# Results of the stage between two loops: kept in tiles that outlive its pools, stored from the sync queue, the dO store first

## The chip, the cores and the metric

One core of a Trainium2 chip runs the whole kernel in one launch. The metric is the device time of the program in microseconds. The core has five engines that run beside each other: TensorE (PE, matmuls), VectorE (DVE), ScalarE (ACT), GpSimd (POOL) and SyncE (SP), which here issues transfers only. Transfers (DMA) are issued into a queue by SP, ACT or POOL and carried out by 16 DMA engines.

## The reference

The kernel computes the forward pass and all gradients of one transformer block with conditional layer norms: 2048 tokens, width D = 512, 32 heads of 16, a hidden layer of 1792 with a squared ReLU.

```
mod = silu(c) @ w_mod                       # six rows: sa, ca, ga, sb, cb, gb
h   = layernorm(x) * (1 + ca) + sa
q, k, v = h @ wqkv                          # 32 heads
o   = softmax(q k^T / 4) v
x1  = x + ga * (o @ wo)
h2  = layernorm(x1) * (1 + cb) + sb
out = x1 + gb * (relu(h2 @ w1 + b1)**2 @ w2 + b2)
```

Ten outputs leave the kernel. Those that matter here are out_0 (the result `out`), out_3 (the gradient of `wo`, 512 x 512), and sums over all tokens that the gradients of `c` and `w_mod` are made of. The gradient of `wo` is O^T times da, where O is the attention's output for all tokens and da the gradient that reaches `o @ wo`. The gradient that reaches O is called dO.

## The kernel before

The program has four stages, one after the other: the first layer norm with the projection to q, k and v; the **forward loop** over attention, into which the dense work (the two layer norms, the hidden layer and its gradients) of the first three quarters of the tokens is woven; a **stage between the loops**, in which the last quarter (512 tokens, chunk c = 3) goes through the dense work with nothing beside it; and the **backward loop** over attention, 64 pairs of blocks, each block with sixteen exponentials, followed by the last weight gradients.

The stage between the loops is `last_chunk`. Its order is written out by hand (`manual_schedule`): each engine runs its instructions in the order of the code. Work can be put off: `later(lag, f, ...)` adds an entry to the list `due`, to be done `lag` ticks on, and `tick()`, called between groups of matmuls, runs what has come due. `run_due(True)` at the end runs all that is left. `sp(to, fro)` issues a transfer on the sync queue, in the order of these calls. [...]

What the stage leaves, in the order in which the arithmetic makes it:

- `dOs_c`, the dO of this chunk, token-major; four transposes (DMA) turn it into `dOT`, and `store_grad` stores `dOT` in `dOT_st` and the softmax correction `dlt`, transposed to `dltT`, in `d_st`, from where later heads of the backward loop load them. The first head's share of the last quarter is made on TensorE instead (`head_do`), so the loop can start without these stores.
- `x1_c` and `xlast`, the result of three and of one token tiles, stored to out_0.
- The gradient of `wo`, in four row blocks (`add_chain` with idx from FC + 4*NS = 34 on). The sum over the first three chunks was kept in DRAM and has been fetched ahead; VectorE adds the last chunk's matmul to it and writes the result to a slot (L381), and a store issued from ScalarE one tick later (L335) brings it to out_3.
- The four row sums, in one PSUM bank (`rsums`), copied by VectorE to `racc` (L1225) and stored as four rows to `rows_st` (L1272). They are needed at the end of the program only.

The tiles live in pools: `wk`, `ffw` (racc, and dwbuf with the slots), `cb` (dOT, x1_c, dOs_c). These pools close with the stage, and the backward loop's pools get the same memory. The framework then makes the first instruction that writes to a new tile wait for all that still reads the old ones, stores included. Such first writers are the exponential that fills `E_u` (L1339), the product `dS_u` (L1353), the DMA transpose into `dsT` (L1366) and POOL's fill of the second head set (L945). Other tiles outlive the stage: `r_inv` (the softmax denominators, not read again after the stage), the first head set (k, v, q, do and `qs`, which is spread into `qz` in this stage and free after that), and the pool `dwr` (`dpad`, `proda`, `xlast`), which is released after the stage for POOL's later use.

[...]

In the backward loop, TensorE makes scores (L1333) in three PSUM banks, ScalarE the exponentials (L1339), TensorE the product dO V^T (L1351), VectorE dS (L1353), SP the transposes of dS (L1366), and TensorE accumulates the gradients of k and v (L1384, L1393) and q (L1411).

Of the kernel before, what the change touches and what calls it, by code (L numbers as in the profile page):

```python
# [17 lines left out]
BF = dt.bfloat16  # L18
F32 = dt.float32

P = 128
D = 512
DC = 4
H = 32
# [3 lines left out]
FC = 14  # L28
# [6 lines left out]
def kernel(  # L35
# [6 lines left out]
    n = A_x.shape[1]  # L42
# [3 lines left out]
    NS = -(-FC // 3)  # L46
# [3 lines left out]
    out0_v = out_0[0].rearrange("(t p) d -> p t d", p=P)  # L50
# [3 lines left out]
    DVE = nc.vector  # L54
    ACT = nc.scalar
    POOL = nc.gpsimd
    SP = nc.sync
# [18 lines left out]
    r_inv = persist.tile([P, TT, H], F32, name="r_inv")  # L76
# [3 lines left out]
    rows_st = dram.tile([11, D], F32, name="rows_st")  # L80
# [10 lines left out]
    dOT_st = dram.tile([D, n], BF, name="dOT_st")  # L91
    m_st = dram.tile([H, n], BF, name="m_st")
    d_st = dram.tile([H, n], BF, name="d_st")
# [51 lines left out]
    with ExitStack() as ph:  # L145
# [135 lines left out]
        for g in range(QC):  # L281
            cols = slice(512 * g, 512 * g + 512)
# [13 lines left out]
    with ExitStack() as ph:  # L296
# [7 lines left out]
        racc = ffw.tile([P, 5, D], F32, name="racc")  # L304
        pools = {}

        def mm():
            return pools["mm"].tile([P, 512], F32, name="pm", tag="pm")
# [18 lines left out]
        def later(lag, f, *args):  # L327
            due.append((unit[0] + lag, f, args))
# [10 lines left out]
        def part_tile(w, idx, load):  # L339
            part = cb.tile([P, 512], F32, name="part", tag="part", bufs=4)  # L340
            if load:
                sp(part[:, 0:w], p_st[idx][:, 0:w])
            return part
# [12 lines left out]
            else:  # L356
                ahead[idx] = part_tile(w, idx, True)[:, 0:w]

        slots = {"p": 0, "r": 0}

        def slot(kind, w):
            i = slots[kind]
            slots[kind] = i + 1
            if kind == "r":
                return L_dw[0][:, 512 * (i % 4):512 * (i % 4) + w]
            lo = 2048 + 768 * (i % 6)
            return L_dw[0][:, lo:lo + 2 * w].bitcast(F32)

        L_dw = []

        def add_chain(c, lag, idx, w, lhs, rhs, dst):
            def run():
                if final[0]:
                    acc = pools["mm"].tile([P, 512], F32, name="pc", tag="pc", bufs=3)
                else:
                    acc = mm()
                for ti in range(4):
                    PE.matmul(acc[:, 0:w], lhs(ti), rhs(ti), start=(ti == 0), stop=(ti == 3))  # L378
                if c == QC - 1:
                    res = slot("r", w)  # L380
                    DVE.tensor_tensor(res, acc[:, 0:w], ahead.pop(idx), ALU.add)  # L381
                    later(1, ACT.dma_start, dst, res)
                    if idx < FC - 4:
                        later(1, fetch_part, idx + 4)
                    elif idx < FC:
                        later(1, fetch_part, idx - FC + 4 + FC + 4 * NS)
                    elif idx + 6 < FC + 4 * NS:
                        later(1, fetch_part, idx + 6)
                    return
                if final[0]:  # L390
                    part = slot("p", w)
                    ACT.activation(part, acc[:, 0:w], AF.Identity)
                else:
                    part = part_tile(w, idx, False)[:, 0:w]
                    DVE.tensor_copy(part, acc[:, 0:w])  # L395
                if c == 0:
                    later(1, sp, p_st[idx][:, 0:w], part)
                else:
                    POOL.dma_start(out=p_st[idx][:, 0:w], in_=part, accum_op=ALU.add)
            return (unit[0] + lag, c, run, idx >= FC + 4 * NS)  # L400
# [271 lines left out]
            else:  # L672
                DVE.tensor_scalar(dlt[:, ti, :], delta[:], -1.0, None, ALU.mult)

        def store_grad(c, lag, dOT, dlt):
            dltT = wk.tile([P, P], BF, name="dltT", tag="dltT", bufs=1)
            later(lag, sp, dltT[:], dlt.rearrange("p t h -> p (t h)"), True)
            cols = slice(512 * c, 512 * c + 512)
            later(lag + 3, sp, dOT_st.rearrange("(b p) n -> p b n", p=P)[:, :, cols], dOT.rearrange("p b t q -> p b (t q)"))
            for ti in range(4):  # L680
                later(lag + 3, sp, d_st[:, 512 * c + ti * P:512 * c + (ti + 1) * P], dltT[H * ti:H * ti + H, :])

        funits = [(qc, hg, kt) for qc in range(QC) for hg in range(HG) for kt in range(TT)]
        fh, fe, fcur, fdone, dense = {}, {}, {}, [], []
# [250 lines left out]
        strm, hsets = [], []  # L935
# [33 lines left out]
        def fill(k):  # L969
            for _ in range(min(k, len(dwq))):  # L970
                next_chain()
# [4 lines left out]
        def last_chunk(O_c, L, w1T, w2T):  # L976
            c = QC - 1
            ts = slice(4 * c, 4 * c + 4)
            g_c, x1_c, gf_c, gfT, w1_nat = (L[key] for key in ("g", "x1", "gf", "gfT", "w1"))
# [71 lines left out]
            dpad = dwr.tile([P, 4, 4, 32], BF, name="dpad")  # L1051
# [61 lines left out]
            dlt = wk.tile([P, 4, H], BF, name="dlt", tag="dlt", bufs=1)  # L1113
# [99 lines left out]
            dOT = cb.tile([P, DC, 4, P], BF, name="dOT", tag="gfT")  # L1213
            for ti in range(4):
                later(1, sp, dOT[:, :, ti, :], dOs_c[:, ti, :], True)
            store_grad(c, 1, dOT, dlt)
            later(1, sp, keep["dOs"][:, ts, :], dOs_c[:])
            later(2, sp, out0_v[:, 4 * c:4 * c + 3, :], x1_c[:, 0:3, :])
            mlp(3, {5: head_do})
            fill(len(dwq))  # L1220
            dwq.extend(add_chain(c, 1, FC + 4 * NS + a, D, lambda ti, a=a: O_c[:, ti, a * P:(a + 1) * P], lambda ti: da_c[:, ti, :],
                                 out_3[a * P:(a + 1) * P, :]) for a in range(DC))
            fill(3)
            flush_sums(True)
            DVE.tensor_copy(racc[0:97, 0, :], pools["rs"][0:97, :])  # L1225
            fill(1)
            sp(out0_v[:, 4 * c + 3, :], xlast[:])
            run_due(True)
# [1 line left out]
        keep = {}  # L1230
        final[0] = True
        with ExitStack() as ph2:
            pools["mm"] = ph2.enter_context(tc.tile_pool(name="psM2", bufs=4, space=bass.MemoryType.PSUM))
            with tc.manual_schedule(engines={PE.engine, ACT.engine, DVE.engine, SP.engine, POOL.engine}):
                pools["rs"] = pools["mm"].tile([P, 512], F32, name="rsums", tag="rs", bufs=1)
                DVE.memset(pools["rs"][:], 0.0)
                unit[0] += 1
                run_due()
                L = loads["L"]
                L_dw.append(ffw.tile([P, FC * D], BF, name="dwbuf", tag="wB"))  # L1240
                vaugpool.release()
                head_set(0)
                DVE.memset(hsets[0]["q"][:], 0.0)
                DVE.memset(hsets[0]["do"][:], 0.0)
                copy_const(hsets[0]["k"][:], 1.0)
                O_c = late_finish()
                sp(L["gfT"].rearrange("p t o q -> p (t o) q"), flat(L["gf"]), True)
                for i in range(4):
                    fetch_part(i)
                att.close()  # L1250
                qzpool = tc.alloc_tile_pool(name="qzpool", bufs=1, side="right")
                qz = [qzpool.tile([P, TT, 4, 32], BF, name="qz0")]
                kpool = tc.alloc_tile_pool(name="kpool", bufs=1, side="right")
                dpool = tc.alloc_tile_pool(name="dpool", bufs=1, side="right")
                dwr = tc.alloc_tile_pool(name="dwr", bufs=1, side="right")
                w2T = kpool.tile([P, DC, FF], BF, name="w2T_1", tag="ks")
                for s in range(4):
                    sp(w2T[:, s, :], w2T_st[:, s, :])
                w1T = dpool.tile([P, FC, D], BF, name="w1T_1", tag="dt")
                for s in range(7):  # L1260
                    sp(w1T[:, 2 * s:2 * s + 2, :], w1T_st[:, 2 * s:2 * s + 2, :])

                def head_loads():
                    done = slice(0, 512 * (QC - 1))
                    for i, (to, fro) in enumerate(list(kvq_loads(0)) + list(row_loads(hsets[0]["do"][:, done], dOT_st, 0, done, d_st))):
                        later(i, sp, to, fro)
                    later(12, copy_const, qz[0].rearrange("p t h d -> p (t h d)"), 0.0)
                    later(16, spread_qz, 0)

                last_chunk(O_c, L, w1T, w2T)  # L1270
                for j, row in ((0, 5), (1, 3), (2, 4), (3, 2)):
                    SP.dma_start(out=rows_st[row:row + 1, :], in_=racc[32 * j:32 * j + 1, 0, :])  # L1272
        dwr.release()

    KS_tok, dOs_tok = keep["KS"], keep["dOs"]
# [11 lines left out]
    with ExitStack() as ph:  # L1287
# [162 lines left out]
        with tc.manual_schedule(engines={PE.engine, ACT.engine, DVE.engine, SP.engine, POOL.engine}):  # L1450
# [3 lines left out]
            for b in range(NU // 4 + 3):  # L1454
                toks, bank = order_t if on_pe(b - 1) else order_n
                for tok in toks:
                    c, i = tok[0], int(tok[1:] or 0)
# [22 lines left out]
                    elif c == "T" and 0 <= b - 1 < NU // 4:  # L1480
                        dst, pt = held.pop(i - 1)
# [9 lines left out]
    with ExitStack() as ph:  # L1491
# [156 lines left out]
        with tc.manual_schedule(engines={PE.engine, ACT.engine, DVE.engine}):  # L1648
            for k, (key, i) in enumerate(order):
                for g in range(2):  # L1650
# [4 lines left out]
                    for ti in range(8):  # L1655
                        t = 8 * g + ti
                        PE.transpose(pt[:, ti, :], xs[key, i][:, t * P:(t + 1) * P], identb[:])
                    if key == "dq":
                        dst = dq_tok[:, 8 * g:8 * g + 8, i * P:(i + 1) * P]
                    else:  # L1660
                        dst = dvk_tok[:, 8 * g:8 * g + 8, i, :]
# [32 lines left out]
            for b in range(3):  # L1694
                for ic in range(DC):
                    dwqkv(b, ic)
                    i = b * DC + ic
# [75 lines left out]
```

## Time and profile before

| | us |
|---|---|
| time, median of 3 runs (2641.7 to 2649.67) | 2642.49 |
| span of the profiled run | 2640.8 |
| TensorE busy | 2375.0 (90%) |
| ScalarE busy | 2322.8 (88%) |
| VectorE busy | 1750.3 (66%) |
| last addition of a wo gradient (L381) starts | 1207.27 |
| first exponential of the backward loop starts | 1213.44 |
| last exponential of the backward loop starts | 2505.3 |

Times within the span are microseconds from its start. A group of instructions is given with its line, engine, operation, tile written and tiles read, its count, its busy time and mean length, and then the time for which its engine stood idle just before it and what ended most of that. In the list of waits a line reads: engine and line that waited, what released it, total, times, longest. In the chain that ended last and in the timeline a line begins with its start and its length. The length of a transfer in the timeline is that of its issue alone; when it has landed is known from the completion records of the trace. Matmul records show their modelled ends.

### The profile page before, as it was taken

To read this page: it belongs to the slowest core of one execution; us is meant where nothing else is said; L and a number is where in the kernel's file an instruction comes from. 1 tells how busy PE (TensorE), PEld (TensorE's weight loads), DVE (VectorE), ACT (ScalarE), POOL (GpSimd) and SP (SyncE) were. 2 spreads that over 40 slices of the span, in tenths; PEclk is the share of its full clock that TensorE was granted. 3 is DMA by queue.
4 is the path that set the end of the run, shared out by engine and by line. 5 is a ranking of instruction groups with operands and counts; after the bars stand their busy time and mean duration, and the time that the engine had idled before them with its cause. 6 is when DMAs were issued, how large, how long until landed. Compare 5 with 4: busy or idle time off the path is not lost.

```text
span 2640.8 us, 48843 instructions
## 1 busy us (share of the span) xinstructions
PE 2375.0 (90%) x18110; PEld 746.7 (28%) x18183; DVE 1750.3 (66%) x2234; ACT 2322.8 (88%) x3594; POOL 362.9 (14%) x369
## 2 busy tenths in 40 slices
PE   6699989988988889898999999999999999999999
PEld 2211112322322222352222222222222222222343
DVE  7101134434444534567989989999998999989962
ACT  4599999998999999745999999999999999999943
POOL 2100010211242123201110101101011010110100
PEclk9755559997999799997989999999999999989999
DMA  8863366336855684888999999999999999999982
GB/s 242 195 153 119 99 155 138 85 111 158 137 103 115 140 146 94 193 254 173 196 199 193 205 194 203 197 194 199 198 202 188 199 187 198 195 189 208 194 242 83
DMA packets 1254801, 453.75 MB, mean 172 GB/s; under 512 B 1130127, under 2 KB 1225363, under 8 KB 1254306
## 3 DMA queue, kind: packets, MB, share of 16 engines
q1 hardware_dynamic: 1226066, 415.24, 80.1%
q0 software_dynamic: 10944, 16.78, 4.4%
q10 hardware_dynamic: 17552, 18.59, 2.5%
q8 instruction: 143, 2.34, 0.4%
q14 instruction: 96, 0.79, 0.1%
HBM read 97.08 MB, written 73.95 MB: 65 GB/s over the span
## 4 chain that ended last, share of the span: by engine, by line
PE 42%; ACT 40%; issue 6%; DVE 5%; DMA 2%; SPq 1%; ACTq 0%; POOL 0%; DVEq 0%; POOLq 0%
ACT E_u L1339 20%; ACT ET L704 16%; PE dqacc L1411 6%; PE psS_A L1333 4%; ACT dsT L1482 3%; PE accVK L1384 3%; PE psST L702 3%; PE psS_C L1333 3%; PE psS_B L1333 2%; PE accVK L1393 2%; PE pm L542 2%; PE pm L378 2%; PE oacc L718 2%; PE pdh L1597 2%; PE pwq L1631 2%
## 5 line engine op out<-in xcount | busy, mean ns | idle before, releaser
L1353 DVE TENSOR_TENSOR dS_u<-psD_u,E_u 128x1024 bf16<-128x1024 f32 x1024 | 1187.8, 1218 | 112.1 <-PE psS_B L1333 40.9
L704 ACT ACTIVATE ET<-psST 128x1024 bf16<-128x1024 f32 x1024 | 945.0, 1286 | 39.1 <-PE psST L702 38.4
L1339 ACT ACTIVATE E_u<-psS_A 128x512 bf16<-128x512 f32 x768 | 503.4, 655 | 28.6 <-DMA rows_st<-racc 12.1
L1339 ACT ACTIVATE E_u<-psS_B 128x512 bf16<-128x512 f32 x768 | 499.4, 650 | 5.4 <-issue 0.9
L702 PE MATMUL psST<-qt_sb,kt_sb 32*128 32x512 bf16 x2048 | 408.4, 464 | 67.7 <-ACT ET L704 33.0
L1351 PE MATMUL psD_u<-iv,ido 32*128 32x512 bf16 x2048 | 424.6, 400 | 0.2
L1339 ACT ACTIVATE E_u<-psS_C 128x512 bf16<-128x512 f32 x512 | 332.5, 649 | 1.5 <-PE psS_B L1333 0.7
L1333 PE MATMUL psS_A<-ik,iq 32*128 32x512 bf16 x768 | 305.7, 398 | 18.7 <-ACT E_u L1339 8.1
L1333 PE MATMUL psS_B<-ik,iq 32*128 32x512 bf16 x768 | 307.8, 401 | 10.4 <-ACT E_u L1339 3.2
L718 PE MATMUL oacc<-ET,vaug 128*32 128x512 bf16 x2048 | 246.7, 472 | 5.3 <-DVE ostage L722 5.3
L1384 PE MATMUL accVK<-dS_u,qz 128*32 128x512 bf16 x2048 | 227.9, 415 | 0.5 <-DVE dS_u L1353 0.3
L1333 PE MATMUL psS_C<-ik,iq 32*128 32x512 bf16 x512 | 196.3, 383 | 32.8 <-ACT dsT L1482 28.6
L1333 PEld LDWEIGHTS <-iq 32*128 32x128 bf16 x2048 | 127.3, 92 | 313.3 <-issue 299.0
L1393 PE MATMUL accVK<-E_u,dOs_tok 128*16 128x512 bf16 x2048 | 213.1, 406 | 0.0
L702 PEld LDWEIGHTS <-kt_sb 32*128 32x128 bf16 x2048 | 90.2, 94 | 399.6 <-issue 388.8
L1429 POOL TENSOR_TENSOR dQacc<-dQacc,dqtmp 128x512 f32<-128x512 f32 x64 | 81.3, 1270 | 881.3 <-ACT dqtmp L1424 881.3
L1411 PE MATMUL dqacc<-dsT,KS_tok 128*32 128x512 bf16 x2048 | 182.1, 465 | 14.0 <-DMA dsT<-dS_u 4.7
L722 DVE COPY ostage<-oacc 128x512 f32<-128x512 f32 x32 | 22.0, 689 | 229.8 <-PE oacc L718 182.1
L395 DVE COPY part<-pm 128x512 f32<-128x512 f32 (+2 forms) x103 | 63.5, 617 | 133.3 <-PE pm L378 126.7
L1482 ACT ACTIVATE dsT<-ptT 128x1024 bf16<-128x1024 bf16 x128 | 147.0, 1148 | 4.0 <-PE ptT L1374 3.8
L1351 PEld LDWEIGHTS <-ido 32*128 32x128 bf16 x2048 | 106.7, 91 | 111.2 <-issue 107.0
L1384 PEld LDWEIGHTS <-qz 128*32 128x32 bf16 x2048 | 60.9, 98 | 244.9 <-issue 231.8
(339 smaller groups left out, 2255.8 us busy)
## 6 DMA issues: line engine op xcount, KB each, us to landing
p_st<-part POOLq DMA_DIRECT2D x36, 256.0 KB, 5.2
kt_sb<-qkT_st SPq DMA_DIRECT2D x128, 64.0 KB
wA<-in_B_w_dram SPq DMA_DIRECT2D x28, 256.0 KB
dsT<-dS_u SPq DMA_TRANSPOSE x448
wB<-w1T_st SPq DMA_DIRECT2D x21, 256.0 KB
wA<-w2T_st SPq DMA_DIRECT2D x21, 256.0 KB
wB<-in_B_w_dram SPq DMA_DIRECT2D x21, 256.0 KB
p_st<-part POOLq DMA_DIRECT2D x25, 192.0 KB, 3.9
```

What stands on the lines that cost most here:

```text
L702: PE.matmul(ps[:, hi, :], kt_sb[r:r + 32, kt * P:(kt + 1) * P], qt_sb[r:r + 32, :], start=True, stop=True, tile_position=(r, 0))
L704: ACT.activation(ET[:, 2 * pair:2 * pair + 2, :], ps[:], AF.Exp, scale=SCALE)
L718: PE.matmul(oacc[32 * hq:32 * hq + 32, :], lhsT, ET[:, hq, :], start=(kt == 0), stop=(kt == TT - 1), tile_position=(0, 32 * hq), skip_grou ...
L1333: PE.matmul(psS[:], st["q"][r:r + 32, qt * P:(qt + 1) * P], st["k"][r:r + 32, kc * 512:kc * 512 + 512], start=True, stop=True, tile_positi ...
L1339: ACT.activation(bst[u][0][:, hq, :], sst.pop((u, hq))[:], AF.Exp, scale=SCALE)
L1351: PE.matmul(psD[:, hi, :], st["do"][r:r + 32, qt * P:(qt + 1) * P], st["v"][r:r + 32, kc * 512:kc * 512 + 512], start=True, stop=True, til ...
L1353: DVE.tensor_tensor(dS_u[:, 2 * pair:2 * pair + 2, :], psD[:], E_u[:, 2 * pair:2 * pair + 2, :], ALU.mult)
L1384: PE.matmul(cur["vk"][32 * hq:32 * hq + 32, :], hst[hg]["qz"][:, qt, hq, :], bst[u][1][:, hq, :], start=(qt == 0), stop=False, tile_positi ...
L1393: PE.matmul(acc[32 * hq:32 * hq + DH, :], dOs_tok[:, qt, (hg * 4 + hq) * DH:(hg * 4 + hq + 1) * DH], E_u[:, hq, :], start=False, stop=(qt ...
L1411: PE.matmul(acc[32 * hq:32 * hq + 32, :], KS_tok[:, kc * 4 + kt, h * DH:h * DH + 32], tT[:, :, hq * 4 + kt, :], start=(kt == 0), stop=(kt ...
L1429: POOL.tensor_tensor(dst2, dst, tmp[:], ALU.add)
L1482: ACT.activation(dst, pt[:], AF.Identity)
```

## The change

Three edits, all in the last microseconds of the stage between the loops.

1. The last results no longer lie in tiles of the closing pools. The four `wo` gradient blocks go to the two halves of the first head set's `qs`, to `dpad` and to a new tile `dwlast` in `dwr`; the row sums go to `r_inv`. A new kind of slot, "w", hands these out from the list `L_late`. The aim is that the first writers of the backward loop don't have to wait for these stores.
2. The stores of the `wo` gradient are issued on the sync queue (`sp`) instead of ScalarE's.
3. In the last chunk the store of `dOT` and those of `dltT` come due one tick after the transposes instead of three more (`more=1`), and the store of the three out_0 tiles comes first, then the copy of `dOs_c`, so that the dO stores are issued ahead of `xlast`, of the `wo` gradient and of the row sums.

```
         def slot(kind, w):
             i = slots[kind]
             slots[kind] = i + 1
+            if kind == "w":
+                return L_late[i]
...
                 if c == QC - 1:
-                    res = slot("r", w)
+                    late = idx >= FC + 4 * NS
+                    res = slot("w" if late else "r", w)
                     DVE.tensor_tensor(res, acc[:, 0:w], ahead.pop(idx), ALU.add)
-                    later(1, ACT.dma_start, dst, res)
+                    later(1, sp if late else ACT.dma_start, dst, res)
...
-        def store_grad(c, lag, dOT, dlt):
+        def store_grad(c, lag, dOT, dlt, more=3):
             dltT = wk.tile([P, P], BF, name="dltT", tag="dltT", bufs=1)
             later(lag, sp, dltT[:], dlt.rearrange("p t h -> p (t h)"), True)
             cols = slice(512 * c, 512 * c + 512)
-            later(lag + 3, sp, dOT_st.rearrange("(b p) n -> p b n", p=P)[:, :, cols], dOT.rearrange("p b t q -> p b (t q)"))
+            later(lag + more, sp, dOT_st.rearrange("(b p) n -> p b n", p=P)[:, :, cols], dOT.rearrange("p b t q -> p b (t q)"))
             for ti in range(4):
-                later(lag + 3, sp, d_st[:, 512 * c + ti * P:512 * c + (ti + 1) * P], dltT[H * ti:H * ti + H, :])
+                later(lag + more, sp, d_st[:, 512 * c + ti * P:512 * c + (ti + 1) * P], dltT[H * ti:H * ti + H, :])
...
-            store_grad(c, 1, dOT, dlt)
+            later(1, sp, out0_v[:, 4 * c:4 * c + 3, :], x1_c[:, 0:3, :])
             later(1, sp, keep["dOs"][:, ts, :], dOs_c[:])
-            later(2, sp, out0_v[:, 4 * c:4 * c + 3, :], x1_c[:, 0:3, :])
+            store_grad(c, 1, dOT, dlt, 1)
             mlp(3, {5: head_do})
             fill(len(dwq))
             dwq.extend(add_chain(c, 1, FC + 4 * NS + a, D, lambda ti, a=a: O_c[:, ti, a * P:(a + 1) * P], lambda ti: da_c[:, ti, :],
                                  out_3[a * P:(a + 1) * P, :]) for a in range(DC))
+            qs = hsets[0]["qs"].rearrange("p t e -> p (t e)")
+            L_late.extend((qs[:, 0:D], qs[:, D:2 * D], dpad.rearrange("p t h d -> p (t h d)"),
+                           dwr.tile([P, D], BF, name="dwlast", tag="proda")[:]))
             fill(3)
             flush_sums(True)
-            DVE.tensor_copy(racc[0:97, 0, :], pools["rs"][0:97, :])
+            keep["sums"] = r_inv.rearrange("p t h -> p (t h)")
+            DVE.tensor_copy(keep["sums"][0:97, :], pools["rs"][0:97, :])
...
                 for j, row in ((0, 5), (1, 3), (2, 4), (3, 2)):
-                    SP.dma_start(out=rows_st[row:row + 1, :], in_=racc[32 * j:32 * j + 1, 0, :])
+                    SP.dma_start(out=rows_st[row:row + 1, :], in_=keep["sums"][32 * j:32 * j + 1, :])
```

More of the change, by code (lines that the diff above doesn't have):

```diff
@@ L357, in fetch_part @@
                 ahead[idx] = part_tile(w, idx, True)[:, 0:w]
-        slots = {"p": 0, "r": 0}
+        slots = {"p": 0, "r": 0, "w": 0}
         def slot(kind, w):
@@ L367, in slot @@
             return L_dw[0][:, lo:lo + 2 * w].bitcast(F32)
-        L_dw = []
+        L_dw, L_late = [], []
         def add_chain(c, lag, idx, w, lhs, rhs, dst):
```

## The prediction

> **What bounds the kernel now.** I read the page first, for where the change can matter at all.
>
> ```profile
> PE 2375.0 (90%) x18110; PEld 746.7 (28%) x18183; DVE 1750.3 (66%) x2234; ACT 2322.8 (88%) x3594; POOL 362.9 (14%) x369
> ...
> L1339 ACT ACTIVATE E_u<-psS_A 128x512 bf16<-128x512 f32 x768 | 503.4, 655 | 28.6 <-DMA rows_st<-racc 12.1
> ```
>
> The span is TensorE and ScalarE work; the edited lines lie in none of the big groups. But the last line, the exponentials of the backward loop, has 28.6 us of idle time before it, of which 12.1 us end with a store of four row sums. The loop cannot start before that store has landed. The list of waits between 1195 and 1225 us shows that this is one wait, and who else stood still with it:
>
> ```profile
> ACT E_u L1339 <- DMA rows_st<-racc: 12.1, 1, 12.1
> ...
> PE psS_A L1333 <- ACT E_u L1339: 6.2, 2, 5.6
> ```
>
> ScalarE waits for the store and TensorE for ScalarE (its score banks are full); VectorE, in the same list, waits 6.9 us for TensorE. These are one gap, not three. The chain that ended last, in order of time, runs through it:
>
> ```profile
> 1207.27 0.69 DVE dwbuf L381
> 1207.98 3.21 DMA out_dram<-dwbuf
> ...
> 1211.76 1.14 DMA rows_st<-racc
> 1213.44 2.56 ACT E_u L1339 x5
> ```
>
> The arithmetic ends at 1207.27 + 0.69 = 1207.96. From there to 1213.44, 5.5 us, everything waits for stores. The timeline of the same stretch tells what the sync queue (SPq) did and when the first scores stood:
>
> ```profile
> 1195.90 5.45 SPq L325 DMA_TRANSPOSE dOT<-dOs_c  x4
> ...
> 1207.69 0.38 SPq L325 DMA_DIRECT2D dOT_st<-dOT  x1
> ...
> 1208.10 0.37 PE L1333 MATMUL psS_A<-ik,iq 32*128 32x512 bf16 x1 [0.95 <-DMA out_dram<-dwbuf]
> ...
> 1208.12 2.44 SPq L325 DMA_DIRECT2D d_st<-dltT  x4
> 1210.67 1.34 SPq L1272 DMA_DIRECT2D rows_st<-racc  x4
> ```
>
> The dO store is issued at 1207.69 though its transposes were issued by 1201.35; the four d_st stores take 2.44 us of issue time and the four row stores come last. The first scores stand at 1208.10 + 0.37 = 1208.47.
>
> **Why the exponential waits at all.** E_u takes memory of pools that close with this stage. The waits written into the built program for the first exponential name the last store of all of racc, dwbuf (three of the four wo gradient results), dOT, x1_c and dOs_c. In the changed build the same instruction names only the dO store, the out_0 store of three tiles, the copy of dOs_c and the four dO transposes: rows_st, d_st and out_3 are gone from its list. So after the change the dO store is the last thing that can hold it.
>
> [...] The completion records of this trace put dOT_st at 1211.28, 3.6 us after its issue[...]. [...] 0.34 us for one out_3 issue on ScalarE, 0.33 us for the out_0 store of the same 128 KB on sync. [...] Here the granted clock is 1.00 until 1210[...].
>
> **The change part by part.**
> *Row sums in r_inv, wo gradients in iqs, dpad and dwlast.* Five VectorE instructions keep their number and shape (0.57 to 0.69 us each) and only write elsewhere. iqs had its last reader at 1176.8 (the copy into qz, 1.05 us) and dpad at 1200.33 (its transposes, 0.39 us), four microseconds ahead of the first write at 1204.87: cost nothing. The waits for old dwbuf stores go; the three results already stood back to back with TensorE (matmuls 1203.10 to 1205.86), so gain nothing.
> *Four out_3 stores from ScalarE to sync.* ScalarE stood idle from 1201.4: no gain there. On sync 4 x 0.34 = 1.4 us, behind the dO store in order, so hidden from it. Ahead of what? Of the four row stores (1.34 us) and of the first dsT transpose of the loop.
> *dO store ahead.* New order on sync: x1_c store, dOs_tok copy, dltT transpose, dO store, d_st, xlast, out_3, rows. From 1201.35: 0.54 + 0.59 + 1.23 = 2.36 (the issue times these have in the timeline of before), so the dO store is issued at 1203.7 and off the queue at 1204.1 (0.38), 4.0 us earlier than before. Its inputs, the transposes, had landed by 1202.57 (completion records). Landing: 384 + 512 + 512 KB pass between 1201.9 and the end. Low end: 3.6 us from issue as before, 1207.3. High end: 1.44 MB at 244 GB/s (1195 to 1200 us) is 5.9 us[...], 1208.8. I take 1207.7, near the 342 GB/s of 1205 to 1207.5. From the landing of the row sums (1212.91) to the exponential (1213.44) there were 0.53 us, so the store allows a start between 1207.8 and 1209.3, 1208.2 as taken.
> *Does something else hold it?* Yes: the scores. The first score waits for the last wo gradient result (its PSUM bank), 1207.95, in both builds. Scores stand at 1208.47, exponential some 0.1 us later: 1208.6. So the start is the later of 1208.6 and 1208.2: 1208.6, between 1208.6 and 1209.3.
> *The tail on sync.* d_st wait for dltT, which now follows 896 KB in the queues: about 1206.3. Then 2.44 + 0.33 + 1.4 + 1.34 = 5.5 us: sync is free at 1211.8. The first dsT transpose was issued at 1217.32, 3.9 us after the first exponential; now it is wanted at 1212.5, so it still finds the queue free, with 0.7 us to spare. Its first reader, dqacc, comes two blocks of 16 exponentials later. POOL's fill of the second head set, behind dO, starts earlier; nobody needs it for 100 us.
> *Sum.* 1213.44 - 1208.6 = 4.8 us, 4.1 at the high end of the store. All of it is on the path, since all engines stood in this gap. 2642.5 - 4.7 = **2637.8 us**, 0.18% less.
>
> **What the loop makes of an earlier start.** The clock is the unknown. Windows of 10 us:
>
> ```profile
> 1210.00:1220.00 10.00, 3.68 (x19) 0.79 (x18) 4.32 (x4) 5.54 (x11) 8.54 (x5) 0.56 0.24 54
> 1220.00:1230.00 10.00, 9.12 (x68) 1.96 (x68) 9.39 (x9) 8.15 (x16) 0.25 (x1) 0.67 1.19 181
> 1230.00:1240.00 10.00, 9.94 (x67) 3.14 (x64) 7.86 (x8) 8.98 (x16) 0.00 (x0) 0.50 0.83 171
> 1240.00:1250.00 10.00, 9.70 (x85) 2.30 (x85) 8.10 (x8) 8.18 (x18) 0.00 (x0) 0.73 0.87 154
> 1250.00:1260.00 10.00, 9.33 (x91) 3.25 (x88) 9.89 (x9) 9.96 (x21) 0.00 (x0) 1.00 1.12 201
> ```
>
> After the length come the busy times of PE, its weight loads, DVE, ACT and POOL, then the granted clock, the DMA share and GB/s. The loop starts on a cold array, and from 1220 to 1250 ScalarE is busy 8.15 + 8.98 + 8.18 = 25.3 us where the window at full clock has 3 x 9.96 = 29.9: 4.6 us of exponentials not done. Later, too, every second such window from 1300 to 1390 is at 0.83 (ScalarE 9.2 busy, against 9.9 in those at 1.00). Starts of the exponentials give 19.3 us for a pair of 16-exponential blocks at full clock and 20.4 us with one half-clock window in it: 1.1 us each, for some 45 of 64 pairs. [...]
>
> **The rivals.**
> 1. *The array stays warmer.* The gap of TensorE shrinks from 5.6 us to under 1 us; up to the 4.6 us of the cold start come back as well: 2637.8 - 4.6 = 2633.2. For it: the drop in the clock followed the gap. Against: the first exponentials feed TensorE so thinly (0.91 us busy in 1212.5 to 1215) that the clock may drop all the same, and it fell again in 1228 to 1245 when TensorE was busy.
> 2. *A new wait takes the old one's place.* The dO store, behind 896 KB, lands as late as the row sums did less a microsecond (1211.9 + 0.53 = 1212.4 for the start, 1.0 us won), or the transposes, behind nine late stores, hold the dS buffers; or the loop's clock windows give the time back. Then 2642.5 - 1.0 = 2641.5. [...] Against: the bounds above.
> 3. *Slower.* The shifted phase meets more half-clock windows: 12 more pairs of 64 cost 12 x 1.1 = 13.2, less 4.7: 2651. For it: most pairs are throttled already and the runs of before spread from 2641.7 to 2649.7. Against: three of four executions agree within 1 us.
>
> **How the numbers follow.** The forecast 0.60; rival 1 0.25; rival 2 0.10; rival 3 0.05. The predicted time is the forecast's. The range: 1.5 us below rival 1, since cold start and phase may add up, 2631.5; above, rival 2 and some of the spread of 8 us, 2645. The bound of 0.3% is 7.9 us, 2634.6 to 2650.4. Rival 1 mostly falls below it, and a few of the forecast's cases with a lucky phase: faster 0.29. Rival 3 in its larger half, and what I have not seen: slower 0.05. Same: 0.66.
>
> **What would show it.** Right: the first exponential at 1208.5 to 1209.3 of the same timeline, with its idle time cut from 12.1 to about 7.3 us and ended by a score (or the dO store); the dO store issued near 1203.8; row and out_3 stores issued while exponentials run; the first dsT transpose straight after its dS_u. Wrong: the wait of the first exponential still over 10 us; a wait of sync or VectorE on these stores inside the loop; a start 4.7 us earlier, but a loop from first to last exponential longer or shorter than 1292 us (1213.4 to 2505.3) by over 3 us, with a different share of half-clock windows.

## The result, and the profile after

The changed kernel took 2629.75 us (median of 4 executions, 2628.38 to 2630.95) against 2642.9 us before (4 executions, 2641.7 to 2649.67): ratio 0.9945, 95% interval 0.9927 to 0.9962. That is 13 us less, below the range of the prediction.

More executions give a smaller size. In a later comparison on one chip (e5 below) the same two kernels had medians of 2636.56 us (22 executions, 2629.9 to 2648.3) and 2643.51 us (40 executions, 2633.6 to 2653.2): ratio 0.9972, interval 0.9961 to 0.9984, which is 7.4 us of 2643.5, between 4.2 and 10.3. Single executions of either kernel have a standard deviation of 5 us. The first four of the changed kernel all lie below 2631 us, where only two of the later 22 do, and their mean is 7.2 us below the mean of the 22, three times the standard error of a mean of four (2.4). That is more than chance is likely to give, and most of its cause stays open.

**The wait is gone.** In the page of the changed kernel the group of exponentials that holds the first one no longer names a store (line L1346 is L1339 of before, moved by the edit; the group is that of one score bank of three, 768 of 2048 exponentials):

```profile
span 2628.1 us, 48844 instructions
...
L1346 ACT ACTIVATE E_u<-psS_A 128x512 bf16<-128x512 f32 x768 | 504.7, 657 | 21.7 <-PE psD_u L1358 8.4
```

28.6 us of idle time before the group became 21.7. The timeline of the changed kernel round the start of the loop (start and length, in us; for a transfer, of its issue):

```profile
1202.74 0.54 SPq L325 DMA_DIRECT2D out_dram<-x_c  x1
...
1203.33 0.55 SPq L325 DMA_DIRECT2D dOs_tok<-dOs_c  x1
...
1203.97 1.77 SPq L325 DMA_TRANSPOSE dltT<-dlt  x1
...
1205.92 0.44 SPq L325 DMA_DIRECT2D dOT_st<-dOT  x1
...
1207.13 1.73 SPq L325 DMA_DIRECT2D d_st<-dltT  x4
...
1208.48 0.68 DVE L384 TENSOR_TENSOR dwlast<-pc,part 128x512 bf16<-128x512 f32 x1
...
1209.31 0.37 PE L1340 MATMUL psS_A<-ik,iq 32*128 32x512 bf16 x1 [0.95 <-DMA d_st<-dltT]
...
1209.71 0.60 ACT L1346 ACTIVATE E_u<-psS_A 128x512 bf16<-128x512 f32 x1 [7.15 <-DMA d_st<-dltT]
...
1211.35 1.21 SPq L1279 DMA_DIRECT2D rows_st<-r_inv  x4
...
1213.38 13.57 SPq L1373 DMA_TRANSPOSE dsT<-dS_u  x5
```

The first exponential follows the first score by 0.41 us; before it was 5.34 us (1208.10 to 1213.44). The trace puts the end of its wait on d_st, but d_st is not among the waits of this instruction in the built program, and its last landing, 1209.89, comes after the exponential. The dO store is, and by the completion records it had landed at 1209.02; the scores stood at 1209.68. So the scores are what it waited for. The store came close behind them: ScalarE works off the waits of this exponential as seven instructions one after the other, some 0.08 us apart, and after the store's landing it was through with them at 1209.38, 0.3 us before the scores. The row stores, which held the loop before, are issued at 1211.35, while exponentials run, and the first transpose of dS finds the queue free at 1212.56.

**The other microseconds.** The two traces differ by 2640.8 - 2628.1 = 12.7 us. They divide so: the stage reached its first score 1.2 us *later* in the changed kernel (1209.31 against 1208.10); from there to the first exponential 4.9 us were saved; the first four blocks of the loop took 37.6 instead of 42.2 us (4.6); the rest of the loop 1247.9 instead of 1249.7 (1.8); what follows the loop 133.0 instead of 135.5 (2.5). The second item is what the edit does. The third shows in the windows of 10 us from the first exponential on, of this trace:

```profile
1209.70:1219.70 10.00, 6.82 (x47) 1.46 (x46) 7.95 (x7) 8.47 (x16) 8.56 (x5) 0.67 0.71 162
1219.70:1229.70 10.00, 9.13 (x77) 2.51 (x73) 9.75 (x10) 9.59 (x20) 0.00 (x0) 0.99 1.21 205
1229.70:1239.70 10.00, 8.88 (x102) 3.32 (x100) 9.50 (x9) 9.91 (x19) 0.00 (x0) 1.00 1.05 204
```

The number after POOL's busy time is the granted clock. By the clock records of this trace it is back at full from 1219.8, 10.1 us after the first exponential, and stays there for 71.7 us; before it was between half and 0.73 for some 30 us, with half clock recorded from 1211.3 to 1224.9 and from 1228.4 to 1245.4. From the first exponential to the last the loop took 1285.5 us instead of 1291.9, with 50 half-clock windows instead of 57 (in the clock records of both traces the stretches of half clock in the loop are whole multiples of 3.41 us; one window is 3.41 us); the prediction had named that as a sign against itself. Does it belong to the change? The experiments answer in part.

### The profile page after: what moved, and what is told of

Read it like the earlier page. It is cut to its first block, busy times and chain, and to the rows that moved or that the text cites. A ratio compares the mean times of both kernels' runs of the same rounds, so it can differ in the third digit from the quotient of the medians.

```text
span 2628.1 us, 48844 instructions
## 1 busy us (share of the span) xinstructions
PE 2372.7 (90%) x18110; PEld 747.1 (28%) x18183; DVE 1749.2 (67%) x2234; ACT 2321.5 (88%) x3594; POOL 363.4 (14%) x369
## 4 chain that ended last, share of the span: by engine, by line
PE 42%; ACT 40%; DVE 7%; issue 6%; DMA 3%; SPq 1%; ACTq 0%; DVEq 0%; POOL 0%
ACT E_u L1346 20%; ACT ET L707 15%; PE dqacc L1418 6%; PE psS_A L1340 4%; PE psST L705 3%; ACT dsT L1489 3%; PE accVK L1391 3%; PE psS_C L1340 2%; PE psS_B L1340 2%; PE oacc L721 2%; PE pm L545 2%; PE accVK L1400 2%; PE pdh L1604 2%; PE pm L380 2%; PE pwq L1638 2%
## 5 line engine op out<-in xcount | busy, mean ns | idle before, releaser
L1346 ACT ACTIVATE E_u<-psS_A 128x512 bf16<-128x512 f32 x768 | 504.7, 657 | 21.7 <-PE psD_u L1358 8.4
L1346 ACT ACTIVATE E_u<-psS_B 128x512 bf16<-128x512 f32 x768 | 500.8, 652 | 4.1 <-PE psS_A L1340 0.5
L1346 ACT ACTIVATE E_u<-psS_C 128x512 bf16<-128x512 f32 x512 | 333.0, 650 | 0.6 <-PE psS_B L1340 0.4
```

What stands on the lines that cost most here:

```text
L1346: ACT.activation(bst[u][0][:, hq, :], sst.pop((u, hq))[:], AF.Exp, scale=SCALE)
```

## The experiments

"Theory A" is: earlier start, and a gap that closes also spares the loop its cold start, the half clock of its first 30 us or so. "Theory B": the earlier start alone, the rest is where the half-clock windows happen to fall. Experiments that were timed together (e1 to e4, e5 to e8, e9 to e11, e12 to e15) share the runs of before, on the same chip.

**The tiles alone (e1).** The changed kernel with the two other edits undone:

```
-                    later(1, sp if late else ACT.dma_start, dst, res)
+                    later(1, ACT.dma_start, dst, res)
...
-            later(1, sp, out0_v[:, 4 * c:4 * c + 3, :], x1_c[:, 0:3, :])
+            store_grad(c, 1, dOT, dlt)
             later(1, sp, keep["dOs"][:, ts, :], dOs_c[:])
-            store_grad(c, 1, dOT, dlt, 1)
+            later(2, sp, out0_v[:, 4 * c:4 * c + 3, :], x1_c[:, 0:3, :])
```

> Only the tiles that outlive the pools; the stores of the wo gradient stay on ScalarE, the dO store stays where it was in the order. The first exponential then still waits for the dO store, which is issued near 1207.7 and lands near 1211.3: start near 1211.8, 1.6 us earlier than before. Theory A (start plus cold array: [...]the drop costs 4 to 5 us at the start of the loop): [...]the cold start stays: 2641. Theory B (start alone, the rest of the gain is luck of the clock's phase): 2641. If the tiles were the whole of the gain: 2630.

Measured 2641.75 us, ratio 0.9988 (0.9974 to 1.0001), a gain that is not clear of none. Its timeline:

```profile
1210.99 0.38 SPq L325 DMA_DIRECT2D dOT_st<-dOT  x1
...
1211.60 0.37 PE L1340 MATMUL psS_A<-ik,iq 32*128 32x512 bf16 x1 [0.95 <-DVE dwlast L384]
...
1214.33 0.60 ACT L1346 ACTIVATE E_u<-psS_A 128x512 bf16<-128x512 f32 x1 [9.48 <-DMA d_st<-dltT]
```

2.73 us from score to exponential: in this trace half of the gap is gone, the other half is the dO store, which landed at 1213.92. Why was it issued so late, at 1210.99? The first wo gradient store, issued from ScalarE, landed at 1210.97. The same pair stands in the kernel before: that store's last landing is at 1207.68 and the dO store's issue at 1207.69, and in that trace the dO store's instruction waits on semaphore 101, the one on which the first wo gradient store counts its landings. The list of what the sync queue waited for in before has it too:

```profile
SPq L325 <- DMA out_dram<-dwbuf: 2.3, 1, 2.3
```

Behind the dO store the four d_st stores went out from 1208.12 on. I had not seen this wait when I predicted.

**The order and the queue alone (e2).** Results stay in dwbuf and racc:

```
-                    res = slot("w" if late else "r", w)
+                    res = slot("r", w)
...
-            DVE.tensor_copy(keep["sums"][0:97, :], pools["rs"][0:97, :])
+            DVE.tensor_copy(racc[0:97, 0, :], pools["rs"][0:97, :])
```

> Only the order and the queue: dO stores ahead, wo gradient stores on sync, all results still in tiles of the closing pools. The first exponential waits for the row sums, the last store: start 1212.5 to 1213.5. Both theories: 2642 to 2643. If the early dO store had a worth of its own: under 2638.

2645.2 us, ratio 0.9997 (0.9982 to 1.0012): nothing that the times can tell. The distance was 4.59 us, and the list of waits of this run still has the old line:

```profile
ACT E_u L1345 <- DMA rows_st<-racc: 11.3, 1, 11.3
```

So, by the traces, the tiles are needed for nearly all of the gain, and the order for the second half of it.

**All but the queue (e9).**

```
-                    later(1, sp if late else ACT.dma_start, dst, res)
+                    later(1, ACT.dma_start, dst, res)
```

> The changed kernel with one part undone: the wo gradient stores go back to ScalarE's queue. ScalarE must then issue the last of them, after the last addition, before its first exponential[...]. If the queue matters: the distance from the first score to the first exponential grows from 0.41 us to 1 us or more. If only tiles and order matter: 0.4 to 0.8 us, and the time is that of the changed kernel, 5 to 7 us below before.

2638.97 us against 2646.56, ratio 0.9972 (0.9959 to 0.9985), the ratio of the whole change. The distance was 0.92 us (scores 1207.15, exponential 1208.07), and the wait ended with the landing of the dO store at 1207.97:

```profile
ACT E_u L1346 <- DMA dOT_st<-dOT: 7.7, 1, 7.7
```

It would be wrong to put the half microsecond between 0.92 and 0.41 down to the queue. e12 (below) has the stores on the sync queue and is the changed kernel up to this point, and its distance is 0.88 us: the dO store landed at 1206.64, the scores stood at 1206.54, and ScalarE then had the rest of its waiting instructions to work off. In both traces the transposes of dO began 11.0 and 11.1 us ahead of the first score, against 11.7 to 12.5 in the seven traces with all three edits that show 0.41. So which of the two ends last, scores or dO store, changes from execution to execution by timing that was there before these stores, and no worth of the queue is shown.

**The gap kept warm (e3).** The kernel before, with matmuls on constant data in the gap, whose result nobody reads:

```
                         score(4 * b + i // 4, i % 4, bank[i])
+                        if b == 0 and i == 2:
+                            hot = psx.tile([P, 512], F32, name="hot", tag="accVK")
+                            for _ in range(24):
+                                PE.matmul(hot[:], identb[:], hst[0]["k"][:, 0:512], start=True, stop=True)
```

> The kernel before, with 24 matmuls of 512 columns on constant data behind the first three scores (their result is not read), which keep TensorE busy for 5.2 us of the gap and end before the fourth score can start. The start of the exponentials stays at 1213.4. Theory A: the cold start of 4.6 us goes, the first four blocks take 37.5 us instead of 42.2: 2638. Theory B: 2643.

2645.11 us, ratio 1.0003 (0.9987 to 1.0019). Keeping TensorE busy through the gap did not bring the 4.6 us of theory A: by the interval it won 3.4 us at most. The windows of this run:

```profile
1211.90:1216.90 5.00, 5.00 (x24) 2.18 (x24) 0.00 (x0) 0.01 (x1) 1.97 (x2) 1.00 0.42 139
1216.90:1226.90 10.00, 6.99 (x49) 1.52 (x47) 8.15 (x7) 8.44 (x16) 6.83 (x4) 0.75 0.53 99
1226.90:1236.90 10.00, 9.30 (x70) 2.05 (x66) 9.39 (x8) 8.54 (x17) 0.00 (x0) 0.67 1.15 196
1236.90:1246.90 10.00, 9.84 (x74) 3.12 (x70) 7.28 (x7) 8.26 (x14) 0.00 (x0) 0.50 0.86 155
```

TensorE was busy and at full clock through the gap, and the clock fell all the same once the loop had begun. The first four blocks took 41.8 us. So an idle gap ahead of the loop is not needed for the cold start; the loop's first blocks, with TensorE busy for 6.99 of 10 us, were followed by it all the same.

**The start held back (e4).** The changed kernel with the first exponential done ten times more:

```
                         expo(4 * b + i // 4, i % 4)
+                        if b == 0 and i == 0:
+                            for _ in range(10):
+                                ACT.activation(bst[0][0][:, 0, :], first[:], AF.Exp, scale=SCALE)
```

> The changed kernel, with the first exponential done eleven times in place of once, so that the second follows some 5 us later and TensorE has the idle gap of before again. Theory A: 5 us of delay and most of the cold start of 4.6 us come back: 2637 to 2640. Theory B: the delay alone: 2634.8.

2643.15 us, ratio 0.9995 (0.9981 to 1.0008). The ten took 6.3 us, more than the 5 I had meant, and the first block took 16.9 us against 10.3 in the trace of the changed kernel, 6.6 us more. Against the ratio of the changed kernel, 0.9972, the hold costs 0.0023 of 2645, 6.1 us, with an interval of some 1 to 11. That fits a microsecond of time for a microsecond of start; theory A, scaled to this delay, asked for about 11, which lies at the edge and is not ruled out by this run.

**The first blocks denser (e8).** The kernel before, every score of the first four blocks computed three times (`for _ in range(3)` round the matmul of L1333 where b < 4).

> The kernel before, with every score of the first four blocks computed three times, so that TensorE is denser at the start of the loop. The start stays at the same distance from the scores. Theory A: the second cold stretch of 17 us in blocks two and three goes, the first four blocks take 38 to 40 us and the time falls by 2 to 4.5 us. Theory B: no change, or slower by the repeated work (128 matmuls of 0.2 us, partly in waits).

2660.22 us, ratio 1.0066 (1.0042 to 1.009): slower by 17. The repeated scores sit ahead of the exponentials, the first four blocks took 51.8 us. Half clock did end sooner, 18.4 us after the first exponential instead of 32, but the repeated work cost more than that. A bad experiment for its question.

**More executions and traces (e5, e13, e14, e15).** Both kernels unaltered.

> The changed kernel once more, unaltered, for a second trace and for more executions: before spread from 2637 to 2658 in 59 executions, the change was timed in four. Theory A (earlier start plus a shorter cold start, both in every execution): 9.5 us below before. Theory B (4.9 us of earlier start, the rest was luck of the clock's phase in four executions): 5 us below before. If 13 us is the true size: 13 below.

> The kernel before, unaltered, for another trace. From first score to first exponential 5.2 to 5.4 us. First four blocks: 42 to 42.5 us if the long cold start belongs to the kernel before; anywhere from 37 to 43 us if it is a matter of where the throttle's windows fall.

> As the run before this one: a third trace of the kernel before.

> The changed kernel, unaltered, for a third trace. First score to first exponential 0.41 us. First four blocks 37 to 43 us in either case; two traces gave 37.6 and 42.9.

e5: 2636.56 us, given above. The single executions of e13, e14 and e15 took 2641.5, 2644.0 and 2635.5 us. From the six traces, in us:

| trace | score to exponential | first four blocks | rest of loop | after the loop | half-clock windows in the loop |
|---|---|---|---|---|---|
| before | 5.34 | 42.2 | 1249.7 | 135.5 | 57 |
| before, e13 | 5.63 | 42.2 | 1245.6 | 137.0 | 49 |
| before, e14 | 5.93 | 42.1 | 1249.1 | 135.4 | 57 |
| changed | 0.41 | 37.6 | 1247.9 | 133.0 | 50 |
| changed, e5 | 0.41 | 42.9 | 1243.3 | 133.2 | 51 |
| changed, e15 | 0.41 | 42.5 | 1250.7 | 133.9 | 58 |

Only the first column is nearly the same in each trace of a kernel and far apart between the kernels. What is missing to the spans is the time up to the first score, 1206.2 to 1213.3 us. The short cold start of the first trace did not come again unaltered: e5, e15 and e9 (42.9) start as coldly as before. In the short one the half clock covered 3.3 to 10.1 us after the first exponential, in the long ones also 15 to 33 or so. Why one execution has the second stretch and another not is not shown. In the first 35 us of the loop there are 7 to 17 us of half clock in the traces of the changed kernel, e10, e1 and e4, four of the ten with the moved tiles, and 24 to 31 us in the other six of these and in all six with the old tiles (e8, altered in these blocks, left aside). The windows of e15:

```profile
1206.60:1216.60 10.00, 6.85 (x47) 1.43 (x46) 7.77 (x7) 8.32 (x16) 8.33 (x5) 0.63 0.68 156
1216.60:1226.60 10.00, 9.38 (x67) 1.93 (x66) 9.37 (x9) 8.54 (x17) 0.00 (x0) 0.67 1.13 195
1226.60:1236.60 10.00, 9.84 (x72) 3.11 (x74) 7.57 (x7) 8.49 (x15) 0.00 (x0) 0.50 0.79 153
```

What follows the loop is some 2 us shorter in all three traces of the changed kernel; but e3, with the tail of before, had 132.7, and variants of the changed kernel below had up to 137.5. Over all seventeen traces it goes with the number of half-clock windows that begin in the first 30 us behind the last exponential: 132.7 to 134.0 us with one window (seven traces), 133.9 to 137.0 with two (eight), 137.5 and 138.2 with three (two), and kernels with old and with moved tiles stand in each of these groups.

One more number on record helps: the mean granted clock of every execution. Among executions of the kernel before, 0.001 more of clock comes with 1.0 to 1.3 us less of time (59, 40 and 45 executions, correlation -0.7 to -0.8). In e5 the changed kernel had 0.8873 on average and before 0.8851; in e9 it was 0.8854 and 0.8829, more than twice the standard error in both. The other kernels with moved tiles, e1 and e4, had more clock too (0.8865 and 0.8860 against 0.8842); e2 and e3, without them, did not (0.8834 and 0.8843). With the part of the clock taken out by one straight line for both kernels, the change is worth 4.4 us in e5 and 4.8 in e9 (standard errors of 1), close to what the earlier start is worth in the traces. The other 2 to 3 us go with the higher clock. So theory B falls short: the rest does not look like luck alone. Whether it is the earlier start that raises the clock, by short cold starts that come more often, is not shown.

**The idle times filled (e6, e7).** In both kernels, two of the sixteen scores of every second block computed three times into the same bank, in the places where TensorE idles for 0.43 and 0.47 us:

```
-                        score(4 * b + i // 4, i % 4, bank[i])
+                        score(4 * b + i // 4, i % 4, bank[i], 3 if b > 0 and on_pe(b - 1) and i in (6, 7) else 1)
```

> The kernel before, with two scores of every second block (the seventh and eighth of sixteen) computed three times over into the same bank, same values. They fill the idle time of TensorE, 0.43 and 0.47 us, in the thin window after which the clock drops in most pairs of blocks. If the thin window is what drops the clock, the pairs go from 20.4 to 19.3 us: 45 of 64 by 1.1 us, some 45 us less, 2600. If the drops have another cause: 2645 to 2660.

> The changed kernel with the same repeated scores. With the drops of the clock out of the loop the change stands alone: theory A 9.5 us below the run before this one, theory B 5 us below it.

2633.62 us (ratio 0.9967, 0.9954 to 0.9981) and 2625.41 us (0.994, 0.9918 to 0.9961; 7 executions). Filling the idle times kept the clock up in most pairs: half-clock windows fell from 57 to 31 in e6, and most pairs took 19.3 us. But the drops that are left last longer, mostly two to five windows instead of one, and cost 3 to 5 us each, so that the gain is some 9 us and not 45. The change itself, between the two: 0.0027 of 2643.5, 7 us again, with an interval of roughly 0 to 14.

**Denser still (e10, e11, e12).** The eight transposes of dS on TensorE (`pe_turn`, two groups per second block) done twice into the same bank: both groups (e10), both and the repeated scores (e11), the second group alone (e12, the diff; `* 2` for both groups):

```
-            for i in range(8):
+            for i in tuple(range(8)) * (1 + half):
```

> The changed kernel, with the eight transposes of dS on TensorE (in every second block) done twice into the same bank. They stream 128 rows against the 32 of a score. [...]this lifts the thin window more than the repeated scores did, 20.4 us pairs become 19.3 us pairs, and the time falls 15 to 40 us below the changed kernel. [...]like those, some 10 us below.

> Both: transposes twice and the two scores three times. If more filling is better: below the run before. If TensorE becomes the bound of these blocks: above it.

> The changed kernel with only the second group of eight transposes done twice. Turning both twice took the half-clock windows from 50 to 11 but made a pair 19.8 us for the repeated work. If one repeat is enough for the throttle: pairs of 19.4 to 19.6 us, 5 to 10 us below the run with both, 12 to 18 below the changed kernel. If not enough: between that run and the changed kernel.

2631.57 us (ratio 0.9944, 0.9921 to 0.9967), 2642.2 us (0.9985, 0.9973 to 0.9997) and 2626.1 us (0.992, 0.989 to 0.995; 6 executions). Half-clock windows: 11, 21 and 19. With both groups a pair at full clock takes 19.8 us, with one 19.6: the repeated work has its price. With everything it takes 20.0, and most of the gain is gone; that TensorE is the bound there is likely, but not shown. e12 beats both kernels by its ratios, before by 21 us and the changed kernel by some 14 (5 to 22, from the intervals of two comparisons), and leaves no work out. A pair of its windows (1406 to 1426), and the same pair of the changed kernel below it:

```profile
1406.00:1416.00 10.00, 8.71 (x95) 3.57 (x94) 9.23 (x9) 9.84 (x20) 0.00 (x0) 1.00 1.14 227
1416.00:1426.00 10.00, 9.67 (x96) 2.48 (x92) 9.63 (x10) 9.96 (x21) 0.00 (x0) 1.00 1.18 199
```

```profile
1408.40:1418.40 10.00, 8.96 (x83) 3.04 (x82) 8.16 (x7) 9.11 (x18) 0.00 (x0) 0.83 1.22 208
1418.40:1428.40 10.00, 9.64 (x97) 2.63 (x94) 10.00 (x9) 9.96 (x21) 0.00 (x0) 1.00 1.16 197
```

More matmuls and transposes (191 against 180), and ScalarE has 19.8 us of exponentials in 20 instead of 19.1, while the clock holds.

## Why the prediction was wrong

*What holds the start.* Right. The first exponential waits for the scores, 0.41 us after the first of them; I had said 0.5. The dO store came later than forecast, at 1205.92 and not 1203.7: 1.2 us because this execution reached the stage later, the rest because dltT's transpose took 1.77 us to issue instead of 1.23 and because there are gaps between the issues. It landed 3.1 us after its issue, before the scores, so it cost nothing in this trace; in those of e9 and e12 it came after them and cost half a microsecond, so both of the forecast's bounds, scores and store, are real. (The store's high end, 1208.8, lies 1 us above 1201.9 + 5.9 = 1207.8; that 1 us was an estimate of mine which no trace shows.) Start term forecast 4.8, measured 4.9 in the first pair of traces and 5.2 over three pairs (5.63 on average to 0.41).

*The tail on sync, the new destinations.* Right: sync free 0.8 us ahead of the first transpose of dS (I had said 0.7), no wait on dpad, qs or r_inv.

*The edit to the queue.* Right that ScalarE gains nothing from it. What I missed is that the wo gradient's first store held the dO store back in the kernel before (2.3 us in the sync queue's list); in the changed kernel the dO store is issued at 1205.92, ahead of the first of them at 1209.43. It did not change the number, since the forecast took the new issue time from the new order.

*What the loop makes of an earlier start.* This is the step that failed, by its size: the forecast put everything behind the start at nothing, and rival 1 only "up to the 4.6 us of the cold start". In the traced execution of the first comparison it measured 8.9 us: 4.6 in the first four blocks, 1.8 in the rest of the loop, 2.5 behind it. Over the three pairs of traces it is 4.6 us on average (1.2, 0.8 and 2.6), beside 5.2 for the start and 0.6 lost ahead of the first score. The cause that rival 1 gives does not hold as it stands: e3 filled the gap and won nothing (ratio 1.0003), and e5 and e15 start coldly without a gap. What the runs show in its place is that this part goes with the granted clock of the whole execution, 0.0022 to 0.0025 higher for 2 to 3 us; how the change comes to raise it stays open.

*How the numbers follow.* The range made it worse. Its low end, 2631.5, "1.5 us below rival 1" (1.7 by its own numbers), left nothing for the spread of single executions; above, "some of the spread of 8 us" was allowed for. Over 40 to 59 executions the standard deviation is 5 us. The forecast of 4.7 us is inside the interval that 22 executions give (4.2 to 10.3) and short of its middle, 7.4. A range from the mechanism's ends, 4.1 to 4.8, and 9.3 with rival 1, needed that spread on both sides: with hindsight, some 2627 to 2645. Of the 7.4 us, 5.2 are shown by the traces of the start; the rest goes with the clock. Why the first four executions lay another 6 or 7 us lower is not known: their mean clock, 0.8895 against 0.8873 in the 22, accounts for some 2 us by the slope above.

*One reading.* The line with 28.6 us of idle time, taken for all exponentials of the loop, is that of one score bank of three. The argument rests on the single wait of 12.1 us in it, which is read rightly.

## What to carry to other kernels

When a stage closes its pools, the next stage's first writers inherit waits on the stores out of them, and the last store can set the start, however small or unurgent: here four row stores of 2 KB ended a wait of 12.1 us. Put late results into memory that nobody wants next, and issue first the store whose memory is wanted first: here the first alone closed half of the gap, the second alone about 1 us of it, both together all or nearly all. Before believing a gain of 0.5%, time the kernel often enough to know its spread, and compare the granted clock of the executions: in these kernels about half of the variance goes with it.

## What the runs showed of the hardware

- Three executions within 1 us of each other did not mean a spread of 1 us: 22 to 59 executions of the same kernels spread by 18 to 22 us, standard deviation 4.6 to 5.2.
- A stretch of matmuls that keeps TensorE busy at full clock right up to the loop (5.00 of 5.00 us, clock 1.00) did not keep the clock up once the thin first blocks ran.
- The drop did not need a window without work. In the loops of the traces of before, changed and e5, of the 3.41 us windows at full clock in which TensorE was busy for 70 to 75%, 117 of 139 were followed by half clock; of those busy for 75 to 90%, 2 of 75.
- Repeating work that is already done made the kernel faster: eight extra transposes in every second block, 64 times, took 14 us or so off (5 to 22), with fewer windows at half clock (19 against 50).
- A transfer was held up by another of no relation to it, issued from another engine: the dO store by the first wo gradient store, with 0.01 us (before) and 0.02 us (e1) between the landing of the one and the issue of the other. In the trace of before the instruction of the one waits on the semaphore that the other counts up (101).
- The waits of the first exponential stand in the traces of before and changed as seven instructions of ScalarE one after the other, 0.08 us from one to the next where none of them had to wait: from the landing to the exponential 0.53 us passed in before with six waiting instructions still to come, 0.41 us in e12 with four to come after its own, and 0.10 us in e9, where the wait for the dO store stood last.
